# Luna attention into a squared-ReLU MLP on one core: transposing q and k through the DMA crossbar, re-laying q and v on chip, one ring for the hidden activations, and a fixed TensorE order

## The chip, the cores and the metric

The kernel runs on one core of a Trainium2 chip. Its engines run side by side, each with its own instruction queue: TensorE (PE in the profile; its weight loads are shown apart as PEld), VectorE (DVE), ScalarE (ACT), GpSimd (POOL) and SyncE (SP). POOL and SP issue the transfers here: POOL's queue the loads from main memory, which turn f32 into bf16 on the way, SP's queue the stores of the result. The metric is the device time of one execution in microseconds (us); lower is better.

## The reference

```python
# B=8 batches, H=8 heads, S=576 rows, D=64; p: 32 packing rows per head; w_in 512x2048, w_out 2048x512
def sm_attn(qq, kk, vv):
    s = scale * qq @ kk.T                     # per batch and head
    a = exp(s - max(s));  a = a / (sum(a) + 1e-9)
    return a @ vv
p_packed = sm_attn(p, k, v)                   # 32 rows attend to 576
x = sm_attn(q, p_packed, p_packed)            # 576 rows attend to the 32 packed ones
h = x_as_(4608, 512) @ w_in
out = (s * relu(h)**2 + b) @ w_out            # (4608, 512) f32
```

## The kernel before

Work goes batch by batch. One batch is 576 rows of 8 heads. For a batch the kernel does an **attention** part, an **MLP-in** part and an **out** part.

Attention of batch b (`attention(b)`, cut into 25 pieces by `yield`):
- `pt`: two TensorE transposes of the packing rows, copied by DVE into the block-diagonal `pbd`.
- `tpk`: 24 transposes of k (96 rows x 128 columns each, an even and an odd chunk of one head side by side), four DVE copies into `kT`.
- `s1`: 24 score matmuls, eight exponentials on ACT into `e1`.
- `pp`: 48 half-width matmuls of v against `e1`, and 12 narrow ones for the row sums; DVE copies the result into the block-diagonal `ppbd`.
- `tpq`: 48 half-width transposes of q, four DVE copies into `qT`.
- `scores`, `weights`: second scores, ACT's exponential into `e2`, a matmul with a block of ones for the sums (`dps`), a DVE reciprocal (`rcd`) and a DVE product into `aT`.
- `packed_w`: the packed rows times `w_in`, scaled by `rd` on ACT or DVE, into `pw`. So the MLP's first matrix is folded into the packed rows.

`mlp_in(b)`: 16 steps m, each four matmuls into the two-bank PSUM tile `hps` (128 of the 2048 hidden units), `rlu` on ACT, and its square on DVE into `gT[b]`.

`mlp_out`: 16 accumulating matmuls per 128 rows of output into `yps`, one DVE instruction (`ysb`, with `svec` and `biasrep`), and stores on SP. 576 is 4.5 times 128, so every second batch has one tile whose two halves come from two batches (the straddle tile: two 64-column matmuls per step).

`bias()`: the sum of the 16 row blocks of `w_out` is built by 15 additions on POOL (`wsum`), then one f32 matmul (`cps`) spreads it, and DVE scales it to `biasrep`.

Order: the loop over b weaves `mlp_in(b)`, the out part of b - 1 and the attention of b + 1. The framework's scheduler may still move instructions within each engine's queue. PSUM holds three rings of two buffers: `pst` (one bank, all of attention), `psh` (two banks, `hps`), `psy` (one bank, `yps`). The raw tiles `kn`, `qn`, `vn` have two buffers each, so loads run up to two batches ahead. The first loads on POOL's queue are: k, the packing rows of batch 0, v, q, `w_in`, k, v, q of batch 1, `w_out`, and then the packing rows of all other batches.

"Loop b" below is the pass of the loop over b; a "step" is one m of its sixteen.

Of the kernel before, what the change touches and what calls it, by code (L numbers as in the profile page):

```python
# [11 lines left out]
ALU = mybir.AluOpType  # L12
# [3 lines left out]
def kernel(  # L16
# [17 lines left out]

    nc = tc.nc
# [9 lines left out]
    NC = S // R  # L45
    HP = H // 2
# [7 lines left out]
    TAIL = S - NT * P  # L54

    constp = ctx.enter_context(tc.tile_pool(name="constp", bufs=1))
    wpool = ctx.enter_context(tc.tile_pool(name="wpool", bufs=1))
    qnp = ctx.enter_context(tc.tile_pool(name="qnp", bufs=2))
    knp = ctx.enter_context(tc.tile_pool(name="knp", bufs=2))
    vnp = ctx.enter_context(tc.tile_pool(name="vnp", bufs=2))  # L60
    qtp = ctx.enter_context(tc.tile_pool(name="qtp", bufs=2))
    e1p = ctx.enter_context(tc.tile_pool(name="e1p", bufs=2))
    e2p = ctx.enter_context(tc.tile_pool(name="e2p", bufs=2))
    smp = ctx.enter_context(tc.tile_pool(name="smp", bufs=4))
    ppw = ctx.enter_context(tc.tile_pool(name="ppw", bufs=2))
    gtp = ctx.enter_context(tc.tile_pool(name="gtp", bufs=3))
    ysp = ctx.enter_context(tc.tile_pool(name="ysp", bufs=3))

    pst = ctx.enter_context(tc.tile_pool(name="pst", bufs=2, space=bass.MemoryType.PSUM))
    psy = ctx.enter_context(tc.tile_pool(name="psy", bufs=2, space=bass.MemoryType.PSUM))  # L70
    psh = ctx.enter_context(tc.tile_pool(name="psh", bufs=2, space=bass.MemoryType.PSUM))
# [3 lines left out]
    def load_heads(dst, src, b, h0, h1):  # L75
        nc.gpsimd.dma_start(  # L76
            out=dst[:, h0:h1, :],
            in_=src[b, h0:h1].rearrange("h (r c) d -> r h (c d)", c=NC),
        )
# [12 lines left out]
    def load_p(b0, b1):
        nc.gpsimd.dma_start(
            out=pn[:, b0:b1, :, 0, :],
            in_=p[b0:b1].rearrange("b (q g) j d -> (g j) b q d", g=4),
        )
        nc.vector.tensor_copy(out=pn[:, b0:b1, :, 1, :], in_=pn[:, b0:b1, :, 0, :])
# [12 lines left out]


    load(knp, kn, k, 0, "kn", parts=2)
    identf = constp.tile([P, P], F32, name="identf")
    make_identity(nc, identf)
    identb = constp.tile([P, P], BF16, name="identb")
    nc.vector.tensor_copy(out=identb[:], in_=identf[:])  # L116
# [4 lines left out]
    ones1 = constp.tile([P, 1], BF16, name="ones1")  # L121
    nc.vector.memset(ones1[:], 1.0)
    onesf = constp.tile([P, P], F32, name="onesf")
    nc.vector.memset(onesf[:], 1.0)
    svec = constp.tile([P, 1], F32, name="svec")
    nc.sync.dma_start(out=svec[:], in_=moe_s[0:1].unsqueeze(0).to_broadcast([P, 1]))
    bvec = constp.tile([P, 1], F32, name="bvec")
    nc.sync.dma_start(out=bvec[:], in_=moe_b[0:1].unsqueeze(0).to_broadcast([P, 1]))
    wsum = constp.tile([P, NB], F32, name="wsum")
    biasrep = constp.tile([P, NB], F32, name="biasrep")  # L130
    pbd = [constp.tile([P, NQ, 4, 2, NP], BF16, name=f"pbd{i}") for i in range(2)]
    KW = HS + 32
    kT = [[constp.tile([P, 2, KW], BF16, name=f"kT{i}{hp}") for hp in range(HP)] for i in range(2)]
    ppbd = [constp.tile([P, HP, 2 * NP], BF16, name=f"ppbd{i}") for i in range(2)]
    for i in range(2):
        nc.vector.memset(pbd[i][:], 0.0)
        nc.vector.memset(ppbd[i][:], 0.0)
        for hp in range(HP):
            nc.vector.memset(kT[i][hp][:, :, HS:KW], 0.0)

    load_p(0, 1)
    load(vnp, vn, v, 0, "vn")
    load(qnp, qn, q, 0, "qn")
    for ch in range(NCH):
        load_w_in(ch)
    load(knp, kn, k, 1, "kn")
    load(vnp, vn, v, 1, "vn")
    load(qnp, qn, q, 1, "qn")
    for m in range(0, NFF, 4):
        load_w_out(m, m + 4)  # L150
    load_p(1, B)

    aT, pw = {}, {}
    gT = {}

    def attention(b):
        i = b % 2
        qT = [None] * HP


        pt = pst.tile([P, NQ, P], BF16, tag="t", name="pt", padded_shape=(None, None, 512))
        for qd in range(NQ):
            nc.tensor.transpose(pt[:, qd, :], pn[:, b, qd, :, :], identb[:])  # L163
        for c2 in range(2):
            nc.vector.tensor_copy(  # L165
                out=pbd[i][D * c2:D * c2 + D, :, :, c2, :],
                in_=pt[D * c2:D * c2 + D].rearrange("p q (g j) -> p q g j", g=4),
            )
        yield
        e1 = e1p.tile([R, NQ, NC, 4, NP], BF16, tag="e1", name="e1")  # L170
        for hp in range(HP):
            tp = pst.tile([P, 2, HS], BF16, tag="t", name="tpk", padded_shape=(None, None, 512))
            for h2 in range(2):
                for cp in range(NC // 2):
                    nc.tensor.transpose(  # L175
                        tp[:, h2, cp * R:(cp + 1) * R],
                        kn[b][:, 2 * hp + h2, cp * P:(cp + 1) * P],
                        identb[0:R, 0:R],
                    )
            nc.vector.tensor_copy(out=kT[i][hp][:, :, 0:HS], in_=tp[:])  # L180
            yield
        for hp in range(HP):
            s1 = pst.tile([P, 2, NC, NP], F32, tag="t", name="s1", padded_shape=(None, None, 8, None))
            for h2 in range(2):
                for cp in range(NC // 2):
                    nc.tensor.matmul(  # L186
                        s1[:, h2, 2 * cp:2 * cp + 2, :],
                        kT[i][hp][:, h2, cp * R:cp * R + P],
                        pbd[i][:, hp // 2, 2 * (hp % 2) + h2, :, :],
                        start=(h2 == 0 and cp == 0),  # L190
                        stop=(h2 == 1 and cp == NC // 2 - 1),
                    )
            for h2 in range(2):
                nc.scalar.activation(  # L194
                    out=e1[:, hp // 2, :, 2 * (hp % 2) + h2, :], in_=s1[0:R, h2], func=AF.Exp, scale=scale
                )
            yield
        pp = pst.tile([P, HP * NP + NQ], F32, tag="t", name="pp", padded_shape=(None, 512))
        for hp in range(HP):
            for c in range(NC):  # L200
                for h2 in range(2):
                    nc.tensor.matmul(  # L202
                        pp[D * h2:D * h2 + D, hp * NP:(hp + 1) * NP],
                        vn[b][:, 2 * hp + h2, c * D:(c + 1) * D],
                        e1[:, hp // 2, c, 2 * (hp % 2) + h2, :],
                        start=(c == 0),
                        stop=(c == NC - 1),
                        tile_position=(0, D * h2),
                    )
            yield  # L210
# [174 lines left out]
    for _ in attention(0):  # L385
        pass
# [45 lines left out]
```

## Time and profile before

| | |
|---|---|
| median of 3 runs | 338.32 us (338.02 to 338.54) |
| profiled execution | 338.61 us, of which the span on the core is 336.7 us |
| PE busy | 289.7 us (86%) |
| DVE busy | 218.0 us (65%) |
| ACT busy | 128.8 us (38%) |
| moved by DMA | 28.45 MB |

The profiled execution's time is 1.9 us longer than its span; that difference lies around the core's own work. A busy share is an average: it says how long an engine had work in it, not which engine the end waited for. Matmuls overlap in the pipeline, so how fast TensorE runs is read from the distance between starts in the timeline, not from the duration of one matmul.

### The profile page before, as it was taken

How to read it: one execution, taken by the hardware profiler on the slowest of the kernel's cores; microseconds unless marked ns; L12 is line 12 of the kernel's file. 1: busy time of each engine (PE TensorE's matmuls, PEld its weight loads, DVE VectorE, ACT ScalarE, POOL GpSimd, SP SyncE). 2: the span in 40 equal slices, each digit the busy share in tenths (PEclk: the TensorE clock that was granted, in tenths of full speed). 3: DMA queues.
4: the chain of work that ended last, by engine and by line, in shares of the span. 5: the costliest groups of instructions: out<-in, count | busy, mean ns of one | idle time of the engine just before them, and what ended most of it. 6: DMA issues, size and time to landing. Idle time of an engine off the chain costs nothing.

```text
span 336.7 us, 6310 instructions
## 1 busy us (share of the span) xinstructions
PE 289.7 (86%) x2606; PEld 155.1 (46%) x2642; DVE 218.0 (65%) x395; ACT 128.8 (38%) x257; POOL 45.7 (14%) x56
## 2 busy tenths in 40 slices
PE   0865449636999999999999999999999999999994
PEld 0732237202664456444644465446644653445541
DVE  2449246992754995579767975598559844985311
ACT  1231316600546325450845073615471636335200
POOL 8332002992000001000100001000000000000000
PEclk9999999856999999999999999999999999999998
DMA  8999999700198108821693167511111121021132
GB/s 104 201 206 204 206 184 158 115 0 0 15 148 144 33 22 127 136 56 33 97 147 65 31 101 137 101 33 32 35 31 31 36 55 42 13 76 30 39 88 68
DMA packets 31212, 28.45 MB, mean 84 GB/s; under 512 B 4048, under 2 KB 26576, under 8 KB 31184
## 3 DMA queue, kind: packets, MB, share of 16 engines
q0 software_dynamic: 25136, 18.61, 39.1%
q1 hardware_dynamic: 6048, 9.44, 9.8%
q8 instruction: 20, 0.33, 0.4%
q14 instruction: 8, 0.07, 0.1%
HBM read 37.23 MB, written 9.44 MB: 139 GB/s over the span
## 4 chain that ended last, share of the span: by engine, by line
PE 74%; DMA 11%; POOL 7%; issue 3%; ACT 2%; DVE 1%; POOLq 0%; DVEq 0%; ACTq 0%
PE yps L345 38%; PE hps L305 19%; DMA pn<-in_p_dram 6%; POOL wsum L323 5%; DMA w_in_sb<-in_moe_w_in_dram 5%; PE pw_ps L251 4%; PE tpq L235 3%; PE tpk L175 2%; PE pp L202 2%; PE s L270 2%; PE s L186 1%; ACT rlu L313 1%; PE dps L283 1%; ACT e L194 1%; POOL w_in_sb L100 1%
## 5 line engine op out<-in xcount | busy, mean ns | idle before, releaser
L345 PE MATMUL yps<-w_out_sb,gT 128*128 128x512 bf16 (+1 forms) x604 | 143.9, 382 | 3.7 <-issue 2.8
L313 ACT ACTIVATE rlu<-hps 128x576 bf16<-128x576 f32 x128 | 81.9, 655 | 157.4 <-PE hps L305 153.2
L305 PE MATMUL hps<-aT,pw 128*128 128x288 bf16 x512 | 94.2, 297 | 4.8 <-DVE aT L286 2.5
L314 DVE TENSOR_TENSOR gT<-rlu 128x576 bf16<-128x576 bf16 x128 | 61.8, 488 | 33.9 <-ACT rlu L313 33.2
L345 PEld LDWEIGHTS <-gT 128*128 128x128 bf16 (+1 forms) x640 | 53.5, 100 | 55.9 <-issue 13.8
L285 DVE RECIPROCAL rcd<-dps 128x288 f32<-128x288 f32 x32 | 62.0, 1947 | 9.0 <-PE dps L283 8.9
L305 PEld LDWEIGHTS <-pw 128*128 128x128 bf16 x512 | 45.5, 100 | 33.0 <-issue 15.7
L357 DVE SCALAR_TENSOR_TENSOR ysb<-yps,svec,biasrep 128x512 f32<-128x512 f32 x36 | 26.7, 745 | 20.1 <-PE yps L345 20.1
L251 PE MATMUL pw_ps<-w_in_sb,ppbd 128*64 128x512 bf16 x128 | 28.7, 432 | 5.2 <-DVE pw L263 2.8
L263 DVE TENSOR_SCALAR pw<-pw_ps,rd 128x512 bf16<-128x512 f32 x32 | 22.4, 699 | 12.7 <-PE pw_ps L251 12.7
L261 ACT ACTIVATE pw<-pw_ps,rd 128x512 bf16<-128x512 f32 x32 | 22.0, 687 | 10.5 <-PE pw_ps L251 9.7
L194 ACT ACTIVATE e<-s 96x192 bf16<-96x192 f32 x64 | 17.1, 354 | 11.2 <-PE s L186 10.9
L76 POOL DMA_DIRECT2D kn<-in_k_dram x9 | 7.0, 775 | 101.1 <-PE s L186 69.5
L251 PEld LDWEIGHTS <-ppbd 128*64 128x64 bf16 x128 | 8.9, 111 | 25.3 <-issue 23.7
L240 DVE COPY qT<-tpq 128x576 bf16<-128x576 bf16 x32 | 13.8, 451 | 7.8 <-PE tpq L235 7.5
L278 ACT ACTIVATE e<-s,rs 128x288 bf16<-128x288 f32 x32 | 16.0, 500 | 6.8 <-PE s L270 6.6
L323 POOL TENSOR_TENSOR wsum<-wsum,w_out_sb 128x512 f32<-128x512 f32 x14 | 16.9, 1207 | 1.1
L163 PE MATMUL pt<-identb,pn 128*128 128x128 bf16 x16 | 2.4, 238 | 16.0 <-DVE identb L116 8.6
L175 PE MATMUL tpk<-identb,kn 96*128 96x96 bf16 x192 | 15.1, 224 | 0.8 <-DVE pbd L165 0.8
L180 DVE COPY kT<-tpk 128x576 bf16<-128x576 bf16 x32 | 14.0, 453 | 2.7 <-PE tpk L175 2.3
L286 DVE TENSOR_TENSOR aT<-e,rcd 128x288 bf16<-128x288 bf16 x32 | 15.7, 504 | 0.0
L175 PEld LDWEIGHTS <-kn 96*128 96x128 bf16 x192 | 12.6, 108 | 5.1 <-DVE pbd L165 1.9
(42 smaller groups left out, 143.6 us busy)
## 6 DMA issues: line engine op xcount, KB each, us to landing
vn<-in_v_dram POOLq DMA_DIRECT2D x8, 576.0 KB, 6.9
qn<-in_q_dram POOLq DMA_DIRECT2D x8, 576.0 KB, 6.8
out_dram<-ysb SPq DMA_DIRECT2D x24, 192.0 KB, 2.2
kn<-in_k_dram POOLq DMA_DIRECT2D x7, 576.0 KB, 6.6
out_dram<-ysb SPq DMA_DIRECT2D x24, 128.0 KB, 2.4
w_in_sb<-in_moe_w_in_dram POOLq DMA_DIRECT2D x4, 512.0 KB, 14.1
w_out_sb<-in_moe_w_out_dram POOLq DMA_DIRECT2D x4, 512.0 KB, 21.2
out_dram<-ysb SPq DMA_DIRECT2D x24, 64.0 KB, 2.0
```

What stands on the lines that cost most here:

```text
L175: nc.tensor.transpose(tp[:, h2, cp * R:(cp + 1) * R], kn[b][:, 2 * hp + h2, cp * P:(cp + 1) * P], identb[0:R, 0:R],)
L194: nc.scalar.activation(out=e1[:, hp // 2, :, 2 * (hp % 2) + h2, :], in_=s1[0:R, h2], func=AF.Exp, scale=scale)
L251: nc.tensor.matmul(ps[64 * pr:64 * pr + 64, :], ppbd[i][:, hp, :], w_in_sb[:, hp, ch * NB:(ch + 1) * NB], start=True, stop=True, tile_posi ...
L261: nc.scalar.activation(out=dst, in_=ps[:], func=AF.Copy, scale=rd[:, qd:qd + 1])
L263: nc.vector.tensor_scalar_mul(out=dst, in0=ps[:], scalar1=rd[:, qd:qd + 1])
L285: nc.vector.reciprocal(out=rcd[:], in_=dps[:])
L305: nc.tensor.matmul(hps[:, hf, 0:HS], pw[b][:, qd, m * P:(m + 1) * P], aT[b][:, qd, hf * HS:(hf + 1) * HS], start=(qd == 0), stop=(qd == NQ ...
L313: nc.scalar.activation(out=rlu[:], in_=hps[:, :, 0:HS], func=AF.Relu)
L314: nc.vector.tensor_tensor(out=gT[b][:, m, :].rearrange("p (a s) -> p a s", a=2), in0=rlu[:], in1=rlu[:], op=ALU.mult,)
L323: nc.gpsimd.tensor_tensor(out=wsum[:], in0=wsum[:], in1=w_out_sb[:, m, :], op=ALU.add)
L345: nc.tensor.matmul(yps[i0:i0 + n, :], gT[b][:, m, col:col + n], w_out_sb[:, m, :], start=(m == 0), stop=(m == NFF - 1), tile_position=(0, i0),
L357: nc.vector.scalar_tensor_tensor(out=ysb[:], in0=yps[:], scalar=svec[:], in1=biasrep[:], op0=ALU.mult, op1=ALU.add)
```

## The change

- **Transposes.** k and q of batches 2 to 7 are transposed by one DMA each on SP's queue (`dma_k`, `dma_q`). Batches 0 and 1 still use TensorE (`prep_k`, `prep_q`), q with 24 full-width transposes instead of 48 half-width ones.
- **Re-laid operands.** DVE copies q and v of a batch to chunk-major, head-pair-contiguous tiles `qr`, `vr` (`order_q`, `order_v`). With them `packed` uses 24 full-width matmuls per batch instead of 48 half-width ones.
- **Sums.** The DVE reciprocal of the second softmax becomes a logarithm and an exponential of its negative on ACT, over 576 columns at a time.
- **Ring.** `gT` is one tile with three slots, placed so that the tails of two batches lie side by side; the tile that held two batches becomes one 128-column matmul per step.
- **PSUM.** One ring of three two-bank tiles (`big`) for all but `yps`; evictions are twice as wide.
- **Bias.** 16 bf16 matmuls in the first four steps of loop 1, no POOL sums.
- **Buffers and loads.** `kn`, `qn`, `vn`, `qr`, `vr`, `e1`, `e2` have one buffer each. The packing rows of batches 0 and 1 come right after k of batch 0; those of the others after `w_out`.
- **Order.** Every matmul and transpose keeps its order in the program on TensorE; which step of a loop a piece of attention follows is set by a list `at`. The other engines' queues are still ordered by the scheduler.

```diff
-    qnp, knp, vnp, qtp, e1p, e2p: bufs=2;  gtp: bufs=3;  pst, psh: 2 buffers
+    rawp, attp: bufs=1;  atp, smp, ppw: bufs=2;  psh: 3 tiles of two banks, psy: 2
+    def mm(*a, **kw):
+        return tc.keep_in_program_order(nc.tensor.matmul(*a, **kw))
...
+    gT = wpool.tile([P, NFF, 3 * S], BF16, name="gT")
...
+    load(kn, k, 0, "kn", parts=2)
+    load_p(0, 2)
+    load(qn, q, 0, "qn")
+    load(vn, v, 0, "vn")
...
+    load(kn, k, 1, "kn")
+    load(qn, q, 1, "qn")
+    load(vn, v, 1, "vn")
     for m in range(0, NFF, 4):
         load_w_out(m, m + 4)
-    load_p(1, B)
+    load_p(2, B)
...
+    def by_chunk(dst, src):
+        nc.vector.tensor_copy(
+            out=dst[:].rearrange("r c h d -> r h c d"),
+            in_=src[:].rearrange("r h (c d) -> r h c d", c=NC),
+        )
+    def dma_k(b):
+        nc.sync.dma_start_transpose(
+            out=kT[b % 2][:, 0:H * HS].rearrange("p (x r) -> p x r", r=R),
+            in_=kn[b][:].rearrange("r h x -> r (h x)"),
+        )
+    def order_q(b):
+        qr[b] = attp.tile([R, NC, H, D], BF16, tag="qr", name="qr")
+        by_chunk(qr[b], qn[b])
+    def dma_q(b):
+        nc.sync.dma_start_transpose(
+            out=qT[b % 2][:].rearrange("p c h r -> p (c h) r"),
+            in_=qr[b][:].rearrange("r c h d -> r (c h d)"),
+        )
...
-                    nc.tensor.matmul(pp[D * h2:D * h2 + D, ...], vn[b][:, 2 * hp + h2, ...], ...)
+                mm(pp[:, 0, hp * 2 * NP:(hp + 1) * 2 * NP],
+                    vr[b][:, c, 2 * hp:2 * hp + 2, :], e1[b][:, qd, c, g0:g0 + 2, :], ...)
...
-            nc.vector.reciprocal(out=rcd[:], in_=dps[:])
+        nc.scalar.activation(out=ld[:], in_=dps[:, :, 0:HS], func=AF.Ln)
+        nc.scalar.activation(out=rcd[:], in_=ld[:]..., func=AF.Exp, scale=-1.0)
...
-        nc.gpsimd.tensor_tensor(out=wsum[:], in0=wsum[:], in1=w_out_sb[:, m, :], op=ALU.add)
+        mm(cps[:], onesb[:], w_out_sb[:, m, :], start=(m == 0), stop=(m == NFF - 1))
...
+            at = [0, 1, 3, 4, 6, 8, 9, 10, 12]   # first_scores x2, packed x2, second_scores, packed_w, weights x2, packed_w
...
+            steps.setdefault(11, []).append(lambda: (dma_k(c), order_q(c), dma_q(c)))   # c = b + 2
+            steps.setdefault(14, []).append(lambda: (prep_p(c), order_v(c)))
...
+        for m in range(NFF):
+            mlp_in(b, m)
+            for f in steps.get(m, []):
+                f()
+            if b == 1 and m < 4:
+                for x in range(4):
+                    bias_part(cps, 4 * m + x)
+            run_outs(todo, per)
```

**SP's queue, its first rows.** `svec` and `bvec` are two small constants, `ysb` is a finished block of output. Before:

```order
L126 DMA svec<-in_moe_s_dram 128x1
L128 DMA bvec<-in_moe_b_dram 128x1
L335 DMA out_dram<-ysb 96x512 [waits DVE_49]
L335 DMA out_dram<-ysb 32x512
L335 DMA out_dram<-ysb 64x512 [waits DVE_49]
```

After the change (`kT_111`, `qT_113` serve the even batches, `kT_112`, `qT_114` the odd ones; the first four transposes are those of batches 2 and 3, the last two those of batch 4):

```order
L124 DMA svec<-in_moe_s_dram 128x1
L126 DMA bvec<-in_moe_b_dram 128x1
L231 DMA_TRANSPOSE qT_113<-qr 128x24x96 [waits DVE_49,PE_49]
L199 DMA_TRANSPOSE kT_111<-kn 128x24x96 [waits DMASW2_49]
L231 DMA_TRANSPOSE qT_114<-qr 128x24x96 [waits DVE_49,PE_49]
L199 DMA_TRANSPOSE kT_112<-kn 128x24x96 [waits DMASW6_49]
L401 DMA out_dram<-ysb 96x512 [waits DVE_49]
L401 DMA out_dram<-ysb 32x512
L401 DMA out_dram<-ysb 64x512 [waits DMAHW0_49,DVE_49]
L401 DMA out_dram<-ysb 64x512 [waits DMAHW1_49]
L199 DMA_TRANSPOSE kT_111<-kn 128x24x96 [waits DMAHW2_49,DMAHW3_49,DMASW1_49,PE_49]
L231 DMA_TRANSPOSE qT_113<-qr 128x24x96 [waits PE_49]
```

The stores of loop 1 now share SP's queue with six transposes, four of them ahead of the first store.

**DVE's queue, where loop 0 ends and loop 1 begins.** Before, the last product of batch 1's attention is followed by the bias:

```order
L285 RECIPROCAL rcd<-dps 128x288 [waits PE_49]
L263 TENSOR_SCALAR pw<-pw_ps,rd 128x512 [waits PE_49]
L286 TENSOR_TENSOR aT<-e_751,rcd 128x288 [waits DVE_49]
L326 TENSOR_SCALAR biasrep<-cps,bvec 128x512 [waits DMAHW1_49]
L165 COPY pbd_129<-pt 64x8x32 [waits PE_49]
L314 TENSOR_TENSOR gT<-rlu 128x576 [waits Activation_49]
```

After the change the same place holds the copies `vr` of batch 2 and `qr` of batches 3 and 4:

```order
L165 COPY vr<-vn 96x8x6x64 [waits DMASW3_49]
L384 TENSOR_TENSOR gT<-rlu 128x576 [waits Activation_49]
L358 TENSOR_SCALAR pw<-hps,rd 128x1024 [waits PE_49]
L165 COPY qr<-qn 96x8x6x64 [waits DMAHW2_49,DMASW4_49]
L358 TENSOR_SCALAR pw<-hps,rd 128x1024 [waits PE_49]
L333 TENSOR_TENSOR aT<-e_604,rcd 128x576 [waits Activation_49] x2
L384 TENSOR_TENSOR gT<-rlu 128x576 [waits Activation_49] x2
L165 COPY qr<-qn 96x8x6x64 [waits DMAHW4_49,DMASW7_49,DVE_49]
L384 TENSOR_TENSOR gT<-rlu 128x576 [waits Activation_49] x2
L392 TENSOR_SCALAR biasrep<-yps,bvec 128x512 [waits DMAHW1_49,PE_49]
```

DMAHW2 and DMAHW4 are SP's first and third transposes (q of batches 2 and 3); DMASW4 and DMASW7 are loads of q on POOL's queue. So two copies that belong to batches 3 and 4 stand ahead of `biasrep`, and each waits for the transpose of the batch before it, because `qr` has one buffer.

More of the change, by code (lines that the diff above doesn't have):

```diff
@@ L182, in attention @@
[L182 to L195, printed above, removed]
-                )
-            yield
@@ L320, in bias @@
-    def bias():
-        nc.gpsimd.tensor_tensor(out=wsum[:], in0=w_out_sb[:, 0, :], in1=w_out_sb[:, 1, :], op=ALU.add)
-        for m in range(2, NFF):
-            nc.gpsimd.tensor_tensor(out=wsum[:], in0=wsum[:], in1=w_out_sb[:, m, :], op=ALU.add)
-        cps = psy.tile([P, NB], F32, tag="y", name="cps")
-        nc.tensor.matmul(cps[:], onesf[:], wsum[:], start=True, stop=True)
-        nc.vector.tensor_scalar_mul(out=biasrep[:], in0=cps[:], scalar1=bvec[:])
+                mm(
+                    hps[:, hf, 0:HS],
+                    pw[b][:, qd, m * P:(m + 1) * P],
+                    aT[b][:, qd, hf * HS:(hf + 1) * HS],
+                    start=(qd == 0),
+                    stop=(qd == NQ - 1),
+                )
```

532 lines of the change are left out of this document (307 added, 225 removed).

## The prediction

> **What bounds the kernel now.** I read the page first: span, busy shares, the forty slices.
>
> ```profile
> span 336.7 us, 6310 instructions
> PE 289.7 (86%) x2606; PEld 155.1 (46%) x2642; DVE 218.0 (65%) x395; ACT 128.8 (38%) x257; POOL 45.7 (14%) x56
> ...
> PE   0865449636999999999999999999999999999994
> ```
>
> TensorE (PE) is full from the eleventh slice on and has holes in the first ten (84 us). So there are two stages, a start with gaps and a steady run on PE. The stretches give each its numbers (columns: stretch, length, busy time by engine, PE clock, DMA share, GB/s).
>
> ```profile
> 0.00:46.00 46.00, 22.06 (x208) 13.05 (x208) 20.11 (x50) 11.03 (x22) 16.05 (x26) 1.00 1.23 183
> 59.00:84.00 25.00, 13.35 (x55) 5.42 (x56) 18.41 (x15) 5.96 (x12) 18.09 (x16) 0.66 0.25 38
> 159.50:229.70 70.20, 68.44 (x652) 36.31 (x660) 51.60 (x93) 31.76 (x64) 4.61 (x6) 1.00 0.49 85
> ```
>
> The last is two loops: 35.1 us each, PE 97% busy. PE is idle 24 of the first 46 us and 12 from 59 to 84. The timeline of these stretches says why.
>
> ```profile
> 27.83 0.78 POOL L76 DMA_DIRECT2D kn<-in_k_dram  x1 [2.09 <-DMA kn<-in_k_dram]
> 33.61 0.77 POOL L76 DMA_DIRECT2D qn<-in_q_dram  x1 [2.12 <-DMA qn<-in_q_dram]
> 35.21 1.19 ACT L313 ACTIVATE rlu<-hps 128x576 bf16<-128x576 f32 x2 [7.34 <-PE hps L305]
> 46.32 0.39 DVE L97 COPY pn<-pn 128x896 bf16<-128x896 bf16 x1 [8.12 <-DMA pn<-in_p_dram]
> 78.25 1.22 PE L325 MATMUL cps<-wsum,onesf 128*128 128x512 f32 x1 [6.71 <-POOL wsum L323]
> ```
>
> POOL waits end when batch 1's k lands (27.8) and its q (33.6): two tensors in 5.8 us, 2.9 each, with the loads saturated. Loop 0 starts at 35, DVE then stands 8.1 us until the packing rows land at 46.3, behind `w_out`, and later PE waits for POOL's bias sums until 78.25.
>
> How far before is at 124.15 us: the groups up to there.
>
> ```profile
> L305 PE MATMUL hps<-aT,pw 128*128 128x288 bf16 x139 | 28.7, 326 | 3.6 <-DVE aT L286 2.5 <-ACT rlu L313 1.0
> L345 PE MATMUL yps<-w_out_sb,gT 128*128 128x512 bf16 (+1 forms) x105 | 24.8, 389 | 1.1 <-issue 1.0
> ...
> 328.85 0.75 DVE L357 SCALAR_TENSOR_TENSOR ysb<-yps,svec,biasrep 128x512 f32<-128x512 f32 x1 [2.70 <-PE yps L345]
> 332.30 0.75 DVE L357 SCALAR_TENSOR_TENSOR ysb<-yps,svec,biasrep 128x512 f32<-128x512 f32 x1 [2.70 <-PE yps L345]
> ```
>
> Two batches need 128 `hps` and batch 0's output 64 `yps`, so 11 and 41 belong to loop 2. A `yps` matmul costs 3.45/16 = 0.216 us (the tiles' distance), an `hps` 0.15 (next fence): 1.6 + 8.9 = 10.5 us of loop 2 are done, which began, in effect, at 113.6.
>
> **The steady loops.** Prices are distances between starts.
>
> ```profile
> 195.85 0.42 PE L175 MATMUL tpk<-identb,kn 96*128 96x96 bf16 x6
> 196.11 0.29 PE L305 MATMUL hps<-aT,pw 128*128 128x288 bf16 x1
> 196.24 0.34 PE L186 MATMUL s<-pbd,kT 128*128 128x64 bf16 x6
> 196.41 0.66 PE L305 MATMUL hps<-aT,pw 128*128 128x288 bf16 x4
> ...
> 201.38 0.36 PE L202 MATMUL pp<-e,vn 96*64 96x32 bf16 x12
> 201.68 1.04 PE L345 MATMUL yps<-w_out_sb,gT 128*128 128x512 bf16 x4
> ...
> 203.34 1.02 PE L345 MATMUL yps<-w_out_sb,gT 128*128 128x512 bf16 x4
> 204.30 0.45 PE L235 MATMUL tpq<-identb,qn 96*64 96x96 bf16 x12
> 204.68 0.66 PE L305 MATMUL hps<-aT,pw 128*128 128x288 bf16 x4
> 205.27 0.45 PE L235 MATMUL tpq<-identb,qn 96*64 96x96 bf16 x12
> ```
>
> - Gone from PE: q, four groups of 12 at 0.38 us (204.30 to 204.68), 1.52; k, four of 6 at 0.26, 1.04.
> - `packed`: four groups of 12 at 0.30 become 24 matmuls of 64 columns. The score matmuls have that shape and take 0.17/6 = 0.028 each: 1.20 becomes 0.68, 0.52 less.
> - Straddle tile: 32 half-width matmuls become 16 full ones per two batches. If the halves ran one after the other, 16 x 0.216 = 3.5 us per two batches would go; if side by side, nothing. I take nothing: with the halves side by side the MLP is 16 x (0.59 + 4.5/4 x 0.96) = 26.7 us of a loop, and the 8.4 left are what attention's groups add up to without a remainder of that size.
> - Pinned order, wider evictions, one shared PSUM ring: bounded by the shift of one group switch per step, 0.1 us (an `hps` group takes 0.59 here against 4 x 0.13 at 196.11), so 1.6 us per loop either way; I take 0. A step is 0.59 + 0.96 = 1.55 us on PE, and what it asks of the others is covered by that:
>
> ```profile
> L313 ACT ACTIVATE rlu<-hps 128x576 bf16<-128x576 f32 x128 | 81.9, 655 | 157.4 <-PE hps L305 153.2
> L285 DVE RECIPROCAL rcd<-dps 128x288 f32<-128x288 f32 x32 | 62.0, 1947 | 9.0 <-PE dps L283 8.9
> L263 DVE TENSOR_SCALAR pw<-pw_ps,rd 128x512 bf16<-128x512 f32 x32 | 22.4, 699 | 12.7 <-PE pw_ps L251 12.7
> L180 DVE COPY kT<-tpk 128x576 bf16<-128x576 bf16 x32 | 14.0, 453 | 2.7 <-PE tpk L175 2.3
> L314 DVE TENSOR_TENSOR gT<-rlu 128x576 bf16<-128x576 bf16 x128 | 61.8, 488 | 33.9 <-ACT rlu L313 33.2
> L286 DVE TENSOR_TENSOR aT<-e,rcd 128x288 bf16<-128x288 bf16 x32 | 15.7, 504 | 0.0
> ...
> L323 POOL TENSOR_TENSOR wsum<-wsum,w_out_sb 128x512 f32<-128x512 f32 x14 | 16.9, 1207 | 1.1
> ```
>
> ACT gains four passes of `rlu`'s size per batch (logarithm and exponential), 2.6 us on some 16 per loop, of 32. DVE loses four reciprocals (7.8) and eight copies (3.6) per batch and gains two re-laying copies of 3072 columns. Their price lies between `pn`'s rate (0.39 us for 896 columns: 1.35) and that of `kT` out of PSUM (0.453 for 576: 2.4); I take 1.35, both being SBUF to SBUF in bf16. Neither engine becomes the bound by load. If that cover went (DVE waiting, below), PE would stop once three `rlu` and three `hps` buffers are full.
>
> Sum: 1.52 + 1.04 + 0.52 = 3.1 us per loop, 35.1 to 32.0; five loops (2 to 6) make -15.
>
> **The crossbar transposes.** No row of before shows one. Call the time of one T: 96 x 3072 elements, 576 KB, out as 128 x 24 rows of 96.
>
> ```profile
> q0 software_dynamic: 25136, 18.61, 39.1%
> q1 hardware_dynamic: 6048, 9.44, 9.8%
> ...
> vn<-in_v_dram POOLq DMA_DIRECT2D x8, 576.0 KB, 6.9
> ...
> out_dram<-ysb SPq DMA_DIRECT2D x24, 192.0 KB, 2.2
> ...
> out_dram<-ysb SPq DMA_DIRECT2D x24, 64.0 KB, 2.0
> ```
>
> Low end: the saturated loads' 2.9 us (SP's stores of 64 and 192 KB differ by only 0.2). High end: q1's packets take 0.098 x 16 x 336.7 / 6048 = 0.087 us each, whatever their size (q0's, half as large, 0.084); 3072 rows as packets of their own on 16 engines are 16.7 us. The nearest row is the load of 576 KB, 6.9 us from issue to landing, and I take T = 6.7.
>
> The Trainium skill ("DMA: Bandwidth & Descriptors", § Latency and other measured facts) gives 261 GB/s for a transposing DMA in one kernel, an estimate of 2.3 us for T; the sum below would then be 307. No run so far shows it.
>
> **The start.** The first loads have the same bytes in front of them, so the packing rows still land at 46.3. DVE's queue still holds their copies inside loop 0 (now in step 10), so it waits there as before. Then 2.9 us per tensor: q of batch 2 lands at 49.2, k 52.1, v 55.0, q of batch 3 57.9. DVE's order, listed above, makes this chain:
> - `qr` of batch 2 done at 51 (1.35 after landing, with work in front). First transpose 51 to 51 + T.
> - `vr` of batch 2 at 56.4; a `gT` (0.5) and a `pw` twice as wide as L263's (1.4): 58.2. `qr` of batch 3 waits for the first transpose, 57.7, and its load: done 59.6. A second `pw`, two `aT` (0.7 each, between a `gT` and two of L286): 62.4, and loop 1 begins.
> - `qr` of batch 4 waits for the third transpose (51 + 3T = 71) and for its load, which stands on POOL's queue behind batch 3's k, which waits for the second transpose (51 + 2T = 64.4). Issue 0.8, landing 6.9, and 2.9 behind k: 75. Done 76.4; two `gT` and `biasrep` (0.75, as `ysb`): 78.
> - Meanwhile PE does steps 0 to 3 of loop 1 with the bias matmuls (0.59 + 0.86 + 0.96 each, 9.7) until 72 and 0.6 of step 4, then stands: both `yps` buffers wait for `biasrep`. Loss 5.
> - The rest of loop 1: 12 x 1.55 + 5.3 (attention after the change, 8.4 - 3.1) = 24: 102. The sixth transpose (q of batch 4) waits for the second scores in step 12, some 9 us before that end, so 93 + 6.7, and `qr` of batch 5, `gT`, `pbd` and `aT` behind it push the first step of loop 2 to about 104.
>
> So -9.6 against 113.6. POOL's sums go (17 us of adding), but the chain through SP, DVE and POOL takes their place as the last wait. In loops 2 and 3 DVE again reaches such a copy two steps (3.3 us) after the transpose starts, so it stands 4.8 us; PE's buffers cover two further steps (3.1): 2 us over both loops. Loop 7 and the last five tiles stay.
>
> Sum: -15 - 9.6 + 2 = -22.6. Against the profiled execution, 338.6, that is 316.0; the median lies 0.3 lower, and I leave it at 316. Something within 0.2% (0.7 us) is what a measurement of this kernel can't tell from no change.
>
> **The rivals.**
> - *The transposes' queue decides.* Speaks for it: 3072 short rows, and both packet prices are flat in size. Until loop 2 six transposes stand in a row on SP, so loop 2 starts at 51 + 6T + 5. That passes 128, the start that eats the steady gain too, at T = 12, and with the copies' waits in loops 2 and 3 the sign turns at about T = 10. At 16.7 it starts at 156, and each loop needs 2T = 33.4: 338.6 + 42 - 15 + 5 x 1.4 = 373. Against: a load of the same size takes 6.9.
> - *Block by block.* If the 24 blocks of 128 columns are done one after the other, each at a small store's 2.0 us, T is 48 and SP's queue alone is 51 + 12 x 48, with 61 us of work behind it: 688. Against: 192 KB and 64 KB land within 0.2 us of each other. The Trainium skill ("VectorE: DVE Perf Modes", § The three transpose paths) has 1309 ns for a 128 x 128 square by crossbar against 390 on TensorE; taken in series that is an estimate of 23.6 us for T and 395 us in all, slower than before; no run so far shows such a square.
> - *The pinned order gives the steady gain back.* PE can't step over a group whose operand is late: if each of the 16 steps loses 0.2 us, 3.1 us per loop go, and 338.6 - 9.6 + 2 = 331 remains. For it: attention and `hps` now share three buffers. Against: PE's step is over twice ACT's 0.655.
>
> **How the numbers follow.** Forecast (T from 2.9 to 8.5, 299 to 326; at 2.9 the start costs no wait and the sum is 308): 0.63. Below 299, by more than 1.6 us of switches saved in each loop: 0.05. Pinned order, or T of 8.5 to 10, 326 to 338: 0.12. Queue decides, T above 10, 338 to 373: 0.14. Block by block: 0.06. The range 299 to 345 takes in the first, the third and the lower part of the fourth. Faster is 0.63 + 0.05 + 0.12 less the rim, 0.79; same 0.02; slower 0.19.
>
> **What would show it.** Right: a steady loop near 32 us; no `tpk` and `tpq` after loop 1; PE's longest gap before 90 us ending on a wait for `biasrep` near 78; DVE's idle time before `qr` copies put down to the transposes; these landing near 7 us. Wrong: landings above 12 us, SP's transposes back to back, `qT` or `kT` named as what PE waits for; or a loop of 35 us with PE waiting for `rlu` and `pw`.

## The result and the profile after

The changed kernel takes 314.54 us (median of 4 runs, 314.25 to 316.46) against 338.43 us of the kernel before (4 runs, 338.02 to 338.76): a ratio of 0.9307, 95% interval 0.9268 to 0.9346. It is 7% faster, and the forecast was 316.0. But the sum came out near for the wrong reasons: the start gained nothing where 9.6 us were expected, and a steady loop gained 6.5 us where 3.1 were expected.

The page of the profile after: the span, busy shares, and TensorE and its granted clock over the forty slices.

```profile
span 312.5 us, 4756 instructions
PE 255.1 (82%) x1890; PEld 144.8 (46%) x1920; DVE 146.3 (47%) x291; ACT 140.4 (45%) x209; POOL 28.8 (9%) x40
...
PE   0286868239599469939999799999999999999994
PEclk9999996758799959997999999999999999999999
```

DVE's share fell from 65% to 47%, and TensorE's holes now reach to the 23rd slice (180 us) where before they ended at 84. The stretches show it (length, busy time of PE, PEld, DVE, ACT, POOL, clock, DMA share, GB/s):

```profile
59.00:84.00 25.00, 13.10 (x54) 6.15 (x56) 7.87 (x12) 3.25 (x5) 3.09 (x4) 0.70 1.17 157
84.00:113.00 29.00, 20.91 (x175) 11.73 (x176) 11.50 (x25) 13.93 (x21) 2.30 (x3) 0.91 0.95 148
...
205.00:235.00 30.00, 29.79 (x235) 16.93 (x237) 17.77 (x34) 18.99 (x28) 0.00 (x0) 1.00 0.14 37
```

From 59 to 84 TensorE works as little as before (13.1 of 25 us), with POOL's sums gone; by the slices it is full only from 180 us on, and the last row is such a stretch. In the timeline the start reads as one chain (start, duration, engine, line; in brackets the idle time before it and what ended it; for SP the time is that of issuing):

```profile
49.23 5.68 SPq L231 DMA_TRANSPOSE qT<-qr  x1
54.97 10.50 SPq L199 DMA_TRANSPOSE kT<-kn  x1
64.54 0.95 DVE L165 COPY qr<-qn 96x3072 bf16<-96x3072 bf16 x1 [8.07 <-DMA qT<-qr]
67.41 1.31 PE L72 MATMUL hps<-aT,pw 128*128 128x288 bf16 x4 [10.26 <-DVE aT L333]
80.30 0.96 DVE L165 COPY qr<-qn 96x3072 bf16<-96x3072 bf16 x1 [6.30 <-DMA qn<-in_q_dram]
81.91 0.74 DVE L392 TENSOR_SCALAR biasrep<-yps,bvec 128x512 f32<-128x512 f32 x1
82.71 1.44 PE L72 MATMUL yps<-w_out_sb,gT 128*128 128x512 bf16 x3 [3.24 <-DVE biasrep L392]
...
98.28 2.82 SPq L231 DMA_TRANSPOSE qT<-qr  x1
...
110.25 0.95 DVE L165 COPY qr<-qn 96x3072 bf16<-96x3072 bf16 x1 [8.12 <-DMA qT<-qr]
112.13 1.06 PE L72 MATMUL hps<-w_in_sb,ppbd 128*64 128x512 bf16 x4 [7.01 <-DVE pbd L177]
...
114.81 1.17 PE L72 MATMUL hps<-aT,pw 128*128 128x288 bf16 x4
```

It is the chain that the prediction walked through, link by link, but each link is longer. DVE stands 8.07 us before the copy of batch 3's q until the first transpose has landed, some 15 us after its issue; loop 1 starts at 67.4 after TensorE's longest gap, 10.26 us; the copy for batch 4 waits for a load; the one for batch 5 waits 8.12 us for the sixth transpose, TensorE behind it 7.01. Loop 2's first step is at 114.81, against the 113.6 that the prediction worked out for the kernel before. What waits for what, in sum (us, times, longest):

```profile
PE hps L72 <- DVE aT L333: 12.4, 2, 10.3
PE hps L72 <- DVE pbd L177: 7.0, 1, 7.0
...
DVE qr L165 <- DMA qT<-qr: 27.5, 4, 8.1
DVE qr L165 <- DMA qn<-in_q_dram: 10.1, 4, 6.3
```

The waits of TensorE name DVE's products; DVE's own name the transposes, 27.5 us. The length of a loop is the distance between the first exponentials of attention in it (ACT, the first of two in each of the loops 2 to 6):

```profile
116.65 0.81 ACT L252 ACTIVATE e<-hps 96x768 bf16<-96x768 f32 x1
...
154.40 0.80 ACT L252 ACTIVATE e<-hps 96x768 bf16<-96x768 f32 x1
...
183.03 0.80 ACT L252 ACTIVATE e<-hps 96x768 bf16<-96x768 f32 x1
...
213.34 0.80 ACT L252 ACTIVATE e<-hps 96x768 bf16<-96x768 f32 x1
...
240.20 0.80 ACT L252 ACTIVATE e<-hps 96x768 bf16<-96x768 f32 x1
```

Loop 2 took 37.75 us, loop 3 28.63, and the undisturbed pair after it 30.31 and 26.86 (five and four output tiles): 28.6 on average, where before had 35.1 and the forecast 32.0. The transposes' queue and their median time from issue to landing:

```profile
q1 hardware_dynamic: 34080, 16.52, 27.9%
...
qT<-qr SPq DMA_TRANSPOSE x6, 9.6
kT<-kn SPq DMA_TRANSPOSE x6, 5.5
```

The gain by place, from the two spans: up to loop 2's first step +1.2 us (114.8 against 113.6), after it -25.4 (312.5 - 114.8 = 197.7 against 223.1), together -24.2, which is the difference of the spans.

### The profile page after: what moved, and what is told of

Its sections match the earlier page's. It is cut to its first block, busy times and chain, and to the rows that moved or that the text cites. A ratio compares the mean times of both kernels' runs of the same rounds, so it can differ in the third digit from the quotient of the medians.

```text
span 312.5 us, 4756 instructions
## 1 busy us (share of the span) xinstructions
PE 255.1 (82%) x1890; PEld 144.8 (46%) x1920; DVE 146.3 (47%) x291; ACT 140.4 (45%) x209; POOL 28.8 (9%) x40
## 3 DMA queue, kind: packets, MB, share of 16 engines
q1 hardware_dynamic: 34080, 16.52, 27.9%
## 4 chain that ended last, share of the span: by engine, by line
PE 58%; DMA 10%; DVE 4%; issue 1%; DVEq 0%
PE yps L72 35%; PE hps L72 23%; DMA qT<-qr 10%; DVE gT L384 1%; DVE pw L358 1%; DVE qr L165 0%; DVE ysb L428 0%; DVE aT L333 0%; DVE vr L165 0%; PE hps L75 0%; DVE biasrep L392 0%; DVE ppbd L288 0%; DVE pbd L177 0%; DVEq L165 0%
## 5 line engine op out<-in xcount | busy, mean ns | idle before, releaser
L72 PE MATMUL yps<-w_out_sb,gT 128*128 128x512 bf16 x547 | 141.7, 387 | 5.5 <-DVE biasrep L392 3.2
L382 ACT ACTIVATE rlu<-hps 128x576 bf16<-128x576 f32 x128 | 82.9, 650 | 126.9 <-PE hps L72 125.3
L72 PEld LDWEIGHTS <-gT 128*128 128x128 bf16 x576 | 53.8, 99 | 58.0 <-issue 13.9
L72 PE MATMUL hps<-w_in_sb,ppbd 128*64 128x512 bf16 x128 | 19.4, 424 | 7.4 <-DVE pbd L177 7.0
L165 DVE COPY qr<-qn 96x3072 bf16<-96x3072 bf16 x8 | 7.6, 956 | 37.6 <-DMA qT<-qr 27.5
L358 DVE TENSOR_SCALAR pw<-hps,rd 128x1024 bf16<-128x1024 f32 x16 | 20.4, 1277 | 4.4 <-PE hps L72 4.3
L252 ACT ACTIVATE e<-hps 96x768 bf16<-96x768 f32 x16 | 12.7, 799 | 15.4 <-PE hps L72 15.4
L356 ACT ACTIVATE pw<-hps,rd 128x1024 bf16<-128x1024 f32 x16 | 17.8, 1114 | 0.6 <-PE hps L72 0.6
L72 PE MATMUL hps<-pbd,kT 128*128 128x64 bf16 x192 | 9.2, 202 | 5.6 <-DVE kT L193 5.6
L316 ACT ACTIVATE e<-hps,rs 128x576 bf16<-128x576 f32 x16 | 10.9, 737 | 6.1 <-PE hps L72 5.4
L333 DVE TENSOR_TENSOR aT<-e,rcd 128x576 bf16<-128x576 bf16 x16 | 11.8, 753 | 3.9 <-ACT rcd L332 3.6
L75 PE MATMUL hps<-identb,pn 128*128 128x128 bf16 x16 | 2.4, 239 | 10.4 <-DVE pn L172 8.6
L332 ACT ACTIVATE rcd<-ld 128x576 f32<-128x576 f32 x16 | 10.6, 684 | 0.3
```

The costliest lines, as they stand in the source:

```text
L72: return tc.keep_in_program_order(nc.tensor.matmul(*a, **kw))
L165: nc.vector.tensor_copy(out=dst[:].rearrange("r c h d -> r h c d"), in_=src[:].rearrange("r h (c d) -> r h c d", c=NC),)
L252: nc.scalar.activation(out=e1[b][:, qd].rearrange("r c g j -> r g c j"), in_=s1[0:R].rearrange("r a (g x) -> r (a g) x", g=2)[:, :, 0:NC * ...
L316: nc.scalar.activation(out=e2[b][:, qd, :].rearrange("p (a s) -> p a s", a=2), in_=tiles[qd][:, :, 0:HS], func=AF.Exp, scale=rs[b][:, qd:q ...
L332: nc.scalar.activation(out=rcd[:], in_=ld[:].rearrange("p a s -> p (a s)"), func=AF.Exp, scale=-1.0)
L333: nc.vector.tensor_tensor(out=aT[b][:, qd, :], in0=e2[b][:, qd, :], in1=rcd[:], op=ALU.mult)
```

## The experiments

Theory A was, after this trace: the start is lost because copies of q that belong to later batches stand on DVE's queue in front of work that loop 1 and loop 2 need, and wait there for transposes; the steady gain is larger than forecast because half-width groups cost something at their edges. Ten kernels were run, each in three rounds beside the kernel before (339.38 us beside experiments 1 to 4, 340.56 beside 5, 8, 9 and 10, 339.21 beside 6 and 7; the changed kernel itself ran beside 338.43; between these groups the ratios say more than the differences in us). "Pinned" means kept in the program's order on its engine, as the change does it on TensorE.

**1. The copies pinned on DVE.** The program's order puts `order_q` of batch b + 2 at step 11 (batch 2 in loop 1, step 4); the scheduler had moved it ahead.

```diff
-        nc.vector.tensor_copy(
+        tc.keep_in_program_order(nc.vector.tensor_copy(
             out=dst[:].rearrange("r c h d -> r h c d"),
...
```

> The changed kernel, but the two re-laying copies (qr, vr) may no longer move ahead of the DVE instruction that the program puts before them. Theory A (DVE's queue was the cause: copies of batches 3 and 4 stood ahead of biasrep and of batch 2's products and waited for transposes there): loop 2 starts near 90 us instead of 114, loop 2 loses its 8 us of waiting, loop 3 its 3; 275 to 288 us. Rival B (the transposes themselves are late, whatever the queue): the wait moves to TensorE, which stands at the first scores of batch 2 or at its second scores; within 5 us of the 314.5.

Measured: 288.46 us (287.65 to 288.93), ratio 0.849 (0.8461 to 0.8519). Its timeline (DVE, then the first exponentials of loops 2 to 4):

```profile
76.59 0.75 DVE L392 TENSOR_SCALAR biasrep<-yps,bvec 128x512 f32<-128x512 f32 x1
...
78.81 0.95 DVE L165 COPY qr<-qn 96x3072 bf16<-96x3072 bf16 x1
...
100.32 0.80 ACT L252 ACTIVATE e<-hps 96x768 bf16<-96x768 f32 x1
...
130.63 0.80 ACT L252 ACTIVATE e<-hps 96x768 bf16<-96x768 f32 x1
...
157.49 0.80 ACT L252 ACTIVATE e<-hps 96x768 bf16<-96x768 f32 x1
```

One edit to DVE's order takes 26.1 us off the changed kernel (25.6 by the spans, 27.6 by the ratios). That bears out Theory A, half a us above its range: loop 2's first step is at 99, not near 90. By the first exponentials loop 2 begins 16.3 us earlier (100.32 against 116.65) and loops 2 and 3 take 30.31 and 26.86 us, 9.2 less together. The transposes land no sooner on the whole than in the changed kernel (medians 9.9 and 8.8 us for k and q, against 5.5 and 9.6), and no copy of q waits for one: it was the order that let the transfers cost time. Loop 1 still begins at 66.3, since DVE there stands 9.76 us for packing rows at 46.5.

**2. The same transposes on TensorE.** k and q of all batches through TensorE, the rest of the change kept.

```diff
-            steps.setdefault(11, []).append(lambda: (dma_k(c), order_q(c), dma_q(c)))
+            steps.setdefault(11, []).append(
+                lambda: (prep_k(c, 0), prep_k(c, 1), order_q(c)))
+            steps.setdefault(13, []).append(lambda: (prep_q(c, 0), prep_q(c, 1)))
...
```

> The changed kernel with k and q of every batch transposed on TensorE, none by the crossbar; all else as it is. Theory A (in this kernel the crossbar costs more by its chain in the start than it saves on TensorE): loops 1 to 6 get 48 transposes of 0.04 us each, 2 us per loop, 12 in all; the chain behind biasrep goes (some 23 us) and the waits in loops 2 and 3 (11): 285 to 298 us. Rival B (the crossbar is where the gain came from): 320 us or more.

Measured: 296.85 us (296.70 to 297.34), ratio 0.8742 (0.8715 to 0.8769). So the crossbar as the change schedules it costs 17.7 us against TensorE, and with the copies pinned (experiment 1) it gains 8.4. The loops from 160.95 to 222.56 us average 30.8, 2.2 more than with the crossbar. The copies are not pinned in this run, but that is not what parts it from experiment 1: loop 2's first exponential comes at 99.33 here and at 100.32 there, and the four loops after it take 123.2 us (to 222.56) against 114.3 (to 214.66).

**3. TensorE's order left to the scheduler.**

```diff
-        return tc.keep_in_program_order(nc.tensor.matmul(*a, **kw))
+        return nc.tensor.matmul(*a, **kw)
...
-        return tc.keep_in_program_order(nc.tensor.transpose(*a, **kw))
+        return nc.tensor.transpose(*a, **kw)
```

> The changed kernel without the pin on TensorE's order. Theory A (what makes the steady loops short is that the program emits each group whole, which the scheduler leaves as it is): the loops from loop 3 on stay within 0.5 us of 28.6 on average, the whole within 4 us of 314.5, the difference from the places in loop 0 where the order moves. Rival B (the pin itself makes the loops short): loops of 31 to 33 us, 325 or more.

Measured: 304.05 us (303.66 to 304.84), ratio 0.8948 (0.8915 to 0.8980). The expectation of no more than 4 us missed: it is 10.5 us faster. DVE's timeline says where:

```profile
74.55 0.75 DVE L392 TENSOR_SCALAR biasrep<-yps,bvec 128x512 f32<-128x512 f32 x1 [0.33 <-PE yps L72]
...
78.01 0.96 DVE L165 COPY qr<-qn 96x3072 bf16<-96x3072 bf16 x1 [1.69 <-DMA qn<-in_q_dram]
```

The copy of batch 4's q now stands behind `biasrep`, not ahead of it, and `biasrep` comes 7.4 us earlier. The steady loops have the same length (28.43, 30.31 and 26.85 us from 145.19 to 230.78), and the waits of copies for transposes stay (27.9 us). Pinning TensorE's order neither gains nor costs in the steady loops; it changed what the scheduler did with DVE's queue in loop 1.

**4. The kernel before, with all packing rows loaded early.** Only the loads' order is changed in the kernel before.

```diff
+    load_p(1, B)      # right behind the first packing rows
...
-    load_p(1, B)      # behind w_out
```

> The kernel before with one thing moved: all packing rows are loaded right behind those of batch 0. Theory A (two gates in a row hold the start of before: the packing rows until 46 us, then the bias sums on POOL until 78): loop 0 runs on without its 8 us of waiting, POOL reaches its sums some 8 us sooner, and the time falls by 5 to 10 us, to 328 to 333. Rival B (the sums wait for w_out and POOL's other loads anyway): less than 2 us.

Measured: 330.15 us (329.92 to 331.26), ratio 0.9726 (0.9693 to 0.9759), 9.2 us less than before, as expected. POOL's first sum starts at 51.45 us, where it started at 59.04 in the kernel before:

```profile
51.45 1.16 POOL L321 TENSOR_TENSOR wsum<-w_out_sb 128x512 f32<-128x512 bf16 x1
```

DVE's wait of 8.1 us for the packing rows in loop 0 was on the path, then. The change keeps these rows behind `w_out`, and in experiment 1 DVE still stands 9.76 us for them; experiment 5 goes after that.

**5. The packing rows' copies pinned too.** Experiment 1, and also:

```diff
-        nc.vector.tensor_copy(out=pn[:, b, :, 1, :], in_=pn[:, b, :, 0, :])
+        tc.keep_in_program_order(
+            nc.vector.tensor_copy(out=pn[:, b, :, 1, :], in_=pn[:, b, :, 0, :]))
```

> The kernel of the pinned re-laying copies (288.5 us), with the small copies of the packing rows pinned in DVE's queue too. Theory A (their wait in loop 0, 9.8 us until the rows land behind w_out, is still on the path): TensorE's 9.8 us at the first scores of batch 1 go, loop 1 starts near 57 us instead of 66: 278 to 282 us. Rival B (loop 1 waits for w_out and for batch 2's loads anyway): 286 or more.

Measured: 290.82 us (290.24 to 291.62), ratio 0.8548 (0.8525 to 0.8571): outside what Theory A gave, and by the ratios slower than experiment 1. Loop 1 did begin 11.8 us earlier (54.5 against 66.3). TensorE's waits, and one of them in a steady loop:

```profile
PE hps L75 <- DVE pn L173: 19.5, 8, 9.7
...
84.23 0.96 DVE L165 COPY qr<-qn 96x3072 bf16<-96x3072 bf16 x1 [2.41 <-DMA qn<-in_q_dram]
...
124.53 0.28 PE L75 MATMUL hps<-identb,pn 128*128 128x128 bf16 x2 [1.34 <-DVE pn L173]
```

Pinned right ahead of its two transposes, a copy of 0.2 us stands behind a `gT` that waits for ACT, which waits for TensorE's last step; so TensorE stands 1.34 us in each of the loops, a second time in loop 1 for 2.88, where q's copy waits for its load ahead of it.

**6. Those copies pinned some steps earlier.** Experiment 5 with the copy of batch b + 2 in step 8 of its loop (step 3 in loop 1), its transposes where they were.

```diff
+            steps.setdefault(8, []).append(lambda: copy_p(c))
             steps.setdefault(14, []).append(lambda: (prep_p(c), order_v(c)))
...
+            steps.setdefault(3, []).insert(0, lambda: copy_p(2))
...
```

> As the last version with both kinds of copy pinned (290.82 us), but the packing rows' copy of batch b + 2 is pinned three to six steps ahead of its transposes (step 8 of the loop, step 3 of loop 1) instead of right before them. Theory A (the earlier start of loop 1 was worth its 12 us, and it was lost again because each loop's packing copy stood on DVE's queue behind work that it does not need: TensorE then waited 1.34 us in loops 1 to 6 and 2.88 us in loop 1, and the pause in loop 1 was prolonged by the copy of q that waits for its load): 290.8 less 6 x 1.3 and less 2 to 3 in loop 1 is 279 to 282, and TensorE's waits for pn fall from 19.5 us to under 11. Rival B (loads and transposes set when loop 2 can begin, however early loop 1 starts): 286 to 290, with the waits for pn gone and others, for kT or q's copy, in their place.

Measured: 280.46 us (279.60 to 282.19), ratio 0.8248 (0.8214 to 0.8281), inside what Theory A gave, 10.4 us below experiment 5. TensorE's waits for these copies, and loop 2's first exponential:

```profile
PE hps L75 <- DVE pn L172: 10.0, 2, 9.7
...
93.81 0.80 ACT L255 ACTIVATE e<-hps 96x768 bf16<-96x768 f32 x1
```

The 19.5 us of waits are 10.0, of which 9.7 are the kernel's first load. Loop 2 begins 6.5 us before that of experiment 1, which is the whole difference of their spans (280.4 against 286.9). Of the 11.9 us by which loop 1 began earlier, 5.4 are spent within it; the copy of q there waits 4.3 us for its load.

**7. The copy of q two steps later.** Experiment 6 with `order_q` and `dma_q` in step 13 instead of 11.

```diff
-            steps.setdefault(11, []).append(lambda: (dma_k(c), order_q(c), dma_q(c)))
+            steps.setdefault(11, []).append(lambda: dma_k(c))
+            steps.setdefault(13, []).append(lambda: (order_q(c), dma_q(c)))
...
```

> As the version just before (packing copies pinned early), and the copy of q of batch b + 2 with its transpose goes two steps later, from step 11 to 13, behind the last weights and the last half of the packed rows. Theory A (in loop 1 the copy of q stands on DVE's queue while its load is on the way, and holds the work behind it): 1 to 3 us less than the version before, all of it in loop 1, since in later loops the load is early. Rival B (the transpose of q then lands too late for the second scores in step 6 of the next loop): 2 to 15 us more, with waits of TensorE or DVE for qT in loops 2 to 7.

Measured: 279.37 us (279.16 to 279.45), ratio 0.8223 (0.8197 to 0.8248), the fastest of all. By the medians it is 1.1 us below experiment 6. In the profiled runs it is 2.7 (of experiment 6 that is the slowest run), all of it before loop 2 (first exponential at 91.09 against 93.81), as Theory A had it. The runs of experiment 6 spread over 2.6 us and the intervals overlap, so neither the size nor the gain itself is settled; Rival B's 2 to 15 us more are excluded.

**8 and 9. What a half-width group costs.** Experiment 1 with one more matmul of 32 columns per step in batches 3 to 7 (80 in all), once at full width, once as two halves side by side:

```diff
+        if b >= 3:
+            mm(hps[:, 0, 480:512], pw[b][:, 0, m * P:(m + 1) * P], aT[b][:, 0, 0:32], ...)
```

```diff
+            for pr in range(2):
+                mm(hps[64 * pr:64 * pr + 64, 0, 480:512],
+                    pw[b][:, 0, m * P + 64 * pr:m * P + 64 * pr + 64], aT[b][:, 0, 0:32],
+                    ..., tile_position=(0, 64 * pr))
```

> The kernel of the pinned re-laying copies (288.5 us), with one more full-width matmul of 32 columns behind each hps group of batches 3 to 7 (80 in all, into unused columns of the same PSUM tile; its result is not used). It is the base for the next run. At 0.03 us each (as the 64-column scores) it adds 2.4 us, at 0.1 each 8: 290 to 297.

> As the run before, but the extra matmul is split into two of half the width side by side (80 pairs, results not used). Theory A (the 0.1 us that some groups cost more is paid on the change from a full-width to a half-width group, so fewer such changes are what made the steady loops 3 us shorter than forecast): 80 x 0.09 = 7 us more than the full-width run. Rival B (it is paid on any change of group, and the fixed order saved it): less than 2 us more.

Measured: 290.36 us at full width (289.66 to 290.88), 305.00 as halves (304.76 to 305.40). In the timeline of TensorE, a step's group and the one after it, at full width (5 matmuls in the group):

```profile
185.79 0.67 PE L72 MATMUL hps<-aT,pw 128*128 128x288 bf16 x5
186.31 1.24 PE L72 MATMUL yps<-w_out_sb,gT 128*128 128x512 bf16 x5
```

The same with the halves (6 matmuls):

```profile
186.98 0.79 PE L72 MATMUL hps<-aT,pw 128*128 128x288 bf16 x6
187.70 1.25 PE L72 MATMUL yps<-w_out_sb,gT 128*128 128x512 bf16 x5
```

From the start of this group to that of the next it is 0.52 us against 0.72: 0.20 per pair, and 14.64 / 80 = 0.18 by the medians, twice what Theory A gave. A full matmul more costs (290.36 - 288.46) / 80 = 0.02, so the second half's own work explains little of it. Nor is it what every half-width matmul costs: twelve of them in a row (`pp`, in the prediction's timeline) take 0.30 us. So 0.16 to 0.18 goes into the switch in and out.

**10. The reciprocal back on DVE.** Experiment 1 with the sums inverted by a DVE reciprocal again, over 576 columns at a time where the kernel before took 288.

```diff
-        nc.scalar.activation(out=ld[:], in_=dps[:, :, 0:HS], func=AF.Ln)
...
-        nc.scalar.activation(out=rcd[:], in_=ld[:]..., func=AF.Exp, scale=-1.0)
+        nc.vector.reciprocal(
+            out=rcd[:].rearrange("p (a s) -> p a s", a=2), in_=dps[:, :, 0:HS])
```

> The kernel of the pinned re-laying copies (288.5 us), with the sums' reciprocal on DVE again (over 576 columns at a time) instead of the logarithm and exponential on ACT. Theory A (it was off the path: DVE has some 10 us to spare per loop): within 2 us of 288.5. Rival B (DVE's 3.9 us instruction holds back gT and the evictions, so moving it was part of the gain): 1 to 2 us per loop, 295 to 305.

Measured: 318.83 us (317.94 to 319.97), ratio 0.9371 (0.9341 to 0.9402): 30.4 us more than experiment 1, beyond the numbers of both theories. Its group, DVE's timeline at a loop's end, and a wait of TensorE:

```profile
L330 DVE RECIPROCAL rcd<-hps 128x576 f32<-128x576 f32 x16 | 59.8, 3746 | 4.6 <-PE hps L72 4.6
...
199.49 3.76 DVE L330 RECIPROCAL rcd<-hps 128x576 f32<-128x576 f32 x1 [0.57 <-PE hps L72]
203.17 0.39 DVE L384 TENSOR_TENSOR gT<-rlu 128x576 bf16<-128x576 bf16 x1
...
205.17 3.75 DVE L330 RECIPROCAL rcd<-hps 128x576 f32<-128x576 f32 x1
...
PE hps L72 <- DVE pbd L177: 5.5, 4, 1.7
```

Two reciprocals of 3.75 us stand 5.7 us apart where a step of TensorE takes 1.55, so DVE runs without a pause from 199.5 to 216 and the products queue behind them. Some 12.6 us of the 30 lie in the four loops from loop 2's first exponential to loop 6's (118.17 to 245.07 us, 126.9, against 114.3). There TensorE waits 5.5 us for `pbd`, which stands on DVE's queue behind the reciprocals, and 2.8 for `rlu`; in experiment 1 it waits for no other engine in these loops. The other 18 lie before loop 2. Two reciprocals back to back (67.61, 7.36 us) stand there right ahead of the products for which loop 1 waits, and loop 1 begins 9.4 us later; but the scheduler also ordered DVE's unpinned work otherwise, so how much of the 18 is the reciprocal itself stays open.

## Why the prediction came out as it did

- **Start, -9.6 forecast, +1.2 measured.** The chain was right, its price was not: the step that failed is "the nearest row is the load of 576 KB, 6.9 us from issue to landing, and I take T = 6.7". The first transpose landed after 15 us and the sixth after 12. That the loads are the cause is argued, not shown: they ran beside the chain (a DMA share of 1.17 from 59 to 84, against 0.14 from 205 on), the quickest transposes of the run took 4.8 and 5.7 us (k and q), and no run takes the loads away. So loop 1 began at 67.4 (forecast 62.4), `biasrep` came at 81.9 (78), and loop 2 at 114.8 (104). Experiment 1 shows that it isn't the transfer's length alone: with landings of 9.9 and 8.8 us in the median and the copies in the program's order, loop 2 comes 16.3 us earlier.
- **Waits of the copies in loops 2 and 3, +2 forecast, 9.2 measured.** The 9.2 are 37.75 and 28.63 us against 30.31 and 26.86 in experiment 1. The prediction's own numbers, 4.8 less 3.1 in each loop, give 3.4 and not 2. The rest is the same T again: the two transposes were issued at 128.18 and 164.29, and DVE stood until they had landed, after some 9.8 and 9.4 us:

```profile
138.05 0.96 DVE L165 COPY qr<-qn 96x3072 bf16<-96x3072 bf16 x1 [7.00 <-DMA qT<-qr]
...
173.79 0.96 DVE L165 COPY qr<-qn 96x3072 bf16<-96x3072 bf16 x1 [4.35 <-DMA qT<-qr]
```

  Of these 7.00 and 4.35 us TensorE's buffers covered some: it stood 5.25 and 1.55, so they gave 1.8 and 2.8 where 3.1 was forecast.
- **Steady loop, 32.0 forecast, 28.6 measured.** "Gone from PE" held as far as it went: experiment 2, with k and q on TensorE at full width, costs 2.2 us per loop (1.52 + 1.04 in the forecast, with q at half width). What was mis-sized is an edge price: the prediction bounded it by "the shift of one group switch per step, 0.1 us", 1.6 us per loop, and took 0. The 0.59 that the prediction paid for an `hps` group in every step has 0.1 us in it that is paid only where a half-width group follows. The timeline after shows both, 0.49 ahead of a full group and 0.59 ahead of a half one:

```profile
204.62 0.65 PE L72 MATMUL hps<-aT,pw 128*128 128x288 bf16 x4
205.21 1.05 PE L72 MATMUL hps<-w_in_sb,ppbd 128*64 128x512 bf16 x8
...
207.28 0.65 PE L72 MATMUL hps<-aT,pw 128*128 128x288 bf16 x4
207.77 1.24 PE L72 MATMUL yps<-w_out_sb,gT 128*128 128x512 bf16 x5
```

  The steady timeline of before enters half width some 16.5 times per loop (33 in two loops), that of after 3 times (6 in two). By experiments 8 and 9's 0.16 to 0.18, if every such entry costs as much, that is an estimate of 2.2 to 2.4 of the 3.4 us. No run takes the other 1.1 apart, but the traces show two changes that may be in it. The straddle tile, costed at nothing, took about 4.3 us from start to start in the kernel before (its groups between 182.66 and 188.40) where a full tile takes 3.45: 0.4 us per loop, edges included. And TensorE's idle time in two loops fell from 1.8 us (70.20 less 68.44) to 0.6 (57.17 less 56.62, from 183.03 to 240.20). For the pinned order by itself the 0 held: experiment 3's loops are equal.
- **The reciprocal's move.** "What it asks of the others is covered by that" was right for ACT, which got busier at no cost. But the prediction gave no worth to what left DVE, because DVE at 65% did not look like a bound. Experiment 10 puts some 12.6 us on it in four loops, as a reciprocal of 576 columns. The new kernel's short loops need DVE's products every 1.55 us, and a share over a loop does not show two instructions of 3.75 us.
- **Copies.** 0.956 us each, below the 1.35 to 2.4 that bounded them: a small gain in the chain.
- **The rivals.** "The transposes' queue decides" took its price of a packet as flat, 0.087 us. The rows on q1 give 28032 packets more for 12 transposes, 2336 each of 252 bytes on average, and (0.279 x 312.5 - 0.098 x 336.7) x 16 / 28032 = 0.031 us per packet: 4.5 us for a transpose that has the 16 engines to itself, which is what `kT` nearly shows (median 5.5). The turning point that this rival gave, about T = 10, was in fact passed in the start, though only there; the loops' larger gain paid for it. "Block by block" is excluded by the same 5.5: the Trainium skill ("VectorE: DVE Perf Modes", § The three transpose paths) has 1309 ns for one square, and 18 of them in series would be an estimate of 23.6 us. The 261 GB/s of the Trainium skill ("DMA: Bandwidth & Descriptors", § Latency and other measured facts) does not appear either: 576 KB in 5.5 us are 107 GB/s. "The pinned order gives the steady gain back" is refuted by experiment 3.
- **What would show it.** Held: no transposes of k and q on TensorE after loop 1, and DVE's idle time before the copies put down to the transposes (27.5 us). Not held: the loop near 32, the landings near 7, and TensorE's longest gap ending on `biasrep` (3.24 us there, 10.26 on `aT`). One sign of being wrong did come, landings above 12 us, in the start.

So 316 was near by luck: errors of opposite sign met, +10.8 at the start and +7.2 in the waits of loops 2 and 3, against -17.5 in the five loops (5 x 6.5 = 32.5 gained, without the waits, where 15 were forecast) and, by what is left of the 24.2, -2.1 in loop 7 and the end.

## What to carry to other kernels

When work moves from a matmul engine to DMA, look first at where the instructions that feed the transfer stand on their in-order queue: a copy that waits for the transfer before it holds everything behind it, and here moving a handful of copies a few steps back was worth more (26 us for q's and v's, then 8 for the packing rows') than the 24 us of the whole change. Pin such a copy late enough for its own inputs and early enough for its reader, and not right in front of the reader. Price a matmul group by its neighbour as well as by its size, and read an engine's cover from the stretch where its longest instruction stands, not from its share.

## What the runs showed of the hardware

- A switch of TensorE from full-width groups to 64-column ones and back cost 0.16 to 0.18 us (14.64 us over 80 pairs); ahead of a half-width group 0.1 of it is seen (0.59 against 0.49).
- A crossbar transpose of 96 x 3072 bf16 elements held SP's queue for 2.8 to 10.5 us in issuing (98.28 and 54.97 in the timeline) and went out as 2336 packets of some 252 bytes. A store whose block was done at 129.5 went out at 134.7, behind a transpose that was issued at 128.18 and held the queue for 6.4 us.
- After TensorE had stood still for 10.26 us, the granted clock was 0.50 from 67.41 to 71, 0.82 from 71 to 75 and 1.00 from 75 to 80. The first `hps` group took 1.10 us to the start of the next group (67.41 to 68.51) instead of 0.49 (207.28 to 207.77), so here the gap cost more than its length.
